# Two background streams for a pre-LN attention + MLP decode step with its gradients: groups of heads in one, weight gradients in the other

## The chip, the cores and the metric

One core of a Trainium2 chip. The metric is the device time of one execution in microseconds (us), the median of the runs of a kernel. All profiles quoted here fell in runs of the state "fast", and the ratios use fast runs alone; the medians are over all runs, of which a few are slow (three of 20 of d_two, one of four of d_wq_thin, and one run of the kernel before in three of the calls). One kernel's runs spread by 10 to 20 us, so I quote ratios to the kernel before from the same chip, with their 95% intervals. A ratio is the mean time of one kernel's fast runs over that of the other's of the same rounds, so it is not quite the ratio of the medians that I quote. A "point" is one per cent of the time of the kernel before.

In the profiles PE is the matmul engine (TensorE), PEld its loads of weights, DVE VectorE, ACT ScalarE and POOL GpSimd. The granted clock is the share of PE's full clock that the profile records as granted. Rounds and heads are counted from 0, from the start of a head's score maximum or of its first gV product; the prediction counts p1 heads from 1, so its head 34 is round 33 here.

## The reference, cut to what matters

```python
# B=2, Sq=1, D=640, 32 heads of 128, Sk=4096, Dff=1728; all bf16
def _A_ref(x, k_cache, v_cache, wq, wo):
    q = (x @ wq).reshape(B, Sq, Hq, Dh).transpose(0, 2, 1, 3)
    p = softmax(einsum("bhqd,bhkd->bhqk", q, k_cache) * Dh**-0.5)
    o = einsum("bhqk,bhkd->bhqd", p, v_cache)
    return o.transpose(0, 2, 1, 3).reshape(B, Sq, Hq * Dh) @ wo
h  = x + _A_ref(layernorm(x), k_cache, v_cache, wq, wo)
h2 = h + relu(layernorm(h) @ w1) @ w2
# returned: h2, and by jax.vjp the gradients of x, k_cache, v_cache, wq, wo, w1, w2
```

K and V are 67 MB each and their gradients as much; V is read twice, since the gradient of P needs the gradient of o, which needs the whole forward pass of its batch. In all 372.7 MB move.

## The kernel before: the parts that the change touches

The work on a head is cut into steps. "p1" (66 rounds i) reads K and V, makes the softmax and its sums; "p2" (64 heads j) reads V again (tile W), makes the gradients gV and gK and stores them. Between steps a list of background generators advances; each of their `yield`s has a price, and each step of p1 or p2 adds `rate` to a credit that pays for them. So a higher price makes background work thinner over the foreground.

```python
    bg = []
    done = set()
    credit = [0.0]

    def bg_one():

        while bg:
            try:
                said = next(bg[0][1])
            except StopIteration:
                done.add(bg[0][0])
                bg.pop(0)
                continue
            if isinstance(said, tuple):
                done.add(said)
            return said if isinstance(said, float) else 0.35
        return 0.0

    def bg_step(rate):
        credit[0] = credit[0] + rate if bg else 0.0
        while bg and credit[0] > 0.0:
            credit[0] -= bg_one()

    def bg_until(mark):
        while mark not in done:
            assert bg_one() > 0.0, mark

    M0_ITERS = 11
    P2_AT = H + 2 + M0_ITERS
    RATES = (0.2, 0.5, 0.12, 0.42, 0.88)
    # ... cut: two rounds i for each head j from round P2_AT on, then heads j alone
```

The middle of a batch (row products with wo, w1, w2, then the gradient of the attention output, head by head on VectorE), cut:

```python
    def middle_gen(b):
        # ... cut
        for c in range(ND):
            for h in range(H):
                nc.tensor.matmul(a_ps[:, c:c + 1], lhsT=wo_t[:, h, c * 128:(c + 1) * 128], rhs=OFc[:, h, b:b + 1],
                                 start=(h == 0), stop=(h == H - 1))
                if h % 8 == 7:
                    yield
        # ... cut: layer norm, w1, relu, gradient back to h
        for g in range(H // GH):                 # 4 groups of 8 heads
            for k in range(GH):
                ttr(wo_t[:, g * GH + k, :], hbc[:], go32[:, k:k + 1], D)     # DVE
                yield 0.9
            # ... cut: pr from go32 on DVE
            nc.tensor.matmul(d_ps[:, 0, :], lhsT=ones_f32[:], rhs=pr[:], start=True, stop=True)
            # ... cut
            yield ("go", b, g)                   # head j waits for its group
        # ... cut: product with w2, the row y
        yield ("y", b)
```

The weight gradients, one generator behind the middle of batch 1:

```python
    def fin_gen(fin):
        # ... cut: out_5, out_7, out_6 by outer_rows (matmul of 2-row operands, eviction, store)
        while ("go", 1, H // GH - 1) not in done:
            yield
        yield from rows_of(fin, GQc, H, HD, "GQr")
        yield from rows_of(fin, x1c, ND, D, "x1r")
        yield from outer_rows(fin, FIN["x1r"], D, FIN["GQr"], HD, out_4, ND)
        # ... cut
        for c in range(ND):
            while free["ld"] < 1:
                yield
            st = take("ld", [128, NSC, 128], "wqs")
            nc.sync.dma_start(out=st[:], in_=wqn[:, c, :].rearrange("p (h n) -> p h n", n=128))
            acc = pst([128, B], FP32, "m", "gx_ps")
            for g in range(H // GT):
                t_sb = transpose_group(st, g, g % 2 == 1)
                # ... cut
                yield
                for j in range(GT):
                    h = g * GT + j
                    nc.tensor.matmul(acc[:], lhsT=t_sb[:, j, :], rhs=GQc[:, h, :],
                                     start=(h == 0), stop=(h == H - 1))
                yield
        # ... cut: layer norm back, gradient of x
```

## Time and profile before

| | before |
|---|---|
| time | 1096.96 us median of 3 runs (1096.2 to 1105.84) |
| profiled run | 1104.41 us, trace 1102.6 us, granted clock 0.705 |
| moved | 372.70 MB, mean 338 GB/s |

From the page of the kernel before: the span in 40 equal slices, each digit the busy share in tenths, PEclk the granted TensorE clock in tenths, DMA the busy share of the 16 DMA engines.

```profile
PE   6999888999989878987983863663579788897574
...
PEclk9999899885597988798775565865555555555555
DMA  9999999895475889899899999999679999989835
```

The reader is to see three holes in the DMA row, at slices 10 to 13, around 29, and at the end, and that PE is at 8 or 9 in the first hole. The stretches behind these holes are in the prediction.

### The profile page before, as it was taken

How to read it: one execution, taken by the hardware profiler on the slowest of the kernel's cores; microseconds unless marked ns; L12 is line 12 of the kernel's file. 1: busy time of each engine (PE TensorE's matmuls, PEld its weight loads, DVE VectorE, ACT ScalarE, POOL GpSimd, SP SyncE). 2: the span in 40 equal slices, each digit the busy share in tenths (PEclk: the TensorE clock that was granted, in tenths of full speed). 3: DMA queues.
4: the chain of work that ended last, by engine and by line, in shares of the span. 5: the costliest groups of instructions: out<-in, count | busy, mean ns of one | idle time of the engine just before them, and what ended most of it. 6: DMA issues, size and time to landing. Idle time of an engine off the chain costs nothing.

```text
span 1102.6 us, 32287 instructions
## 1 busy us (share of the span) xinstructions
PE 867.1 (79%) x14111; PEld 748.6 (68%) x14111; DVE 717.6 (65%) x1694; ACT 634.7 (58%) x945; POOL 95.9 (9%) x216
## 2 busy tenths in 40 slices
PE   6999888999989878987983863663579788897574
PEld 5988888888878867876883752553556566554563
DVE  3666777763498876665665677788845665576345
ACT  4555555554566765775762763653367667665343
POOL 0000000000000000000001111111111111111001
PEclk9999899885597988798775565865555555555555
DMA  9999999895475889899899999999679999989835
GB/s 355 374 388 404 410 402 366 290 338 207 159 281 176 287 343 361 330 364 368 344 411 413 360 378 383 369 368 372 278 259 410 409 374 367 365 339 406 333 157 222
DMA packets 59757, 372.70 MB, mean 338 GB/s; under 512 B 5760, under 2 KB 15424, under 8 KB 17376
## 3 DMA queue, kind: packets, MB, share of 16 engines
q1 hardware_dynamic: 38960, 221.50, 53.6%
q0 software_dynamic: 20656, 149.14, 33.3%
q8 instruction: 110, 1.80, 0.6%
q14 instruction: 31, 0.25, 0.1%
HBM read 221.48 MB, written 149.13 MB: 336 GB/s over the span
## 4 chain that ended last, share of the span: by engine, by line
PE 41%; DMA 24%; DVE 17%; issue 10%; ACT 6%; POOL 1%; SPq 0%; POOLq 0%; ACTq 0%; DVEq 0%
PE t_ps L274 17%; DMA out_dram<-gV 10%; PE m_ps L304 9%; DMA Wt<-in_A_v_cache_dram 7%; DVE gK L545 5%; DVE pk L310 4%; PE m_ps L320 3%; PE o_ps L647 3%; ACT t_sb L279 3%; DVE junk L436 3%; PE s_ps L285 3%; DMA out_dram<-ot 2%; DVE gV L545 2%; DMA Vt<-in_A_v_cache_dram 2%; PE dp_ps L285 1%
## 5 line engine op out<-in xcount | busy, mean ns | idle before, releaser
L279 ACT COPY t_sb<-t_ps 128x1024 bf16<-128x1024 bf16 x489 | 490.3, 1014 | 242.8 <-PE t_ps L274 236.5
L274 PE MATMUL t_ps<-ident_bf,Wt 128*128 128x128 bf16 x2048 | 241.7, 291 | 17.3 <-DMA Wt<-in_A_v_cache_dram 16.8
L274 PEld LDWEIGHTS <-Wt 128*128 128x128 bf16 x2048 | 187.2, 133 | 62.3 <-issue 42.9
L285 PEld LDWEIGHTS <-t_sb 128*128 128x128 bf16 x4096 | 171.5, 104 | 61.3 <-ACT t_sb L279 51.2
L310 DVE TENSOR_TENSOR pk<-Kt,ep 128x1024 bf16<-128x1024 bf16 x256 | 174.9, 685 | 47.9 <-ACT ep L353 47.8
L304 PE MATMUL m_ps<-pk,Vt 128*128 128x129 bf16 x2048 | 199.3, 239 | 0.8 <-issue 0.7
L545 DVE TENSOR_TENSOR gV<-rb,pp 128x2048 bf16<-128x2048 bf16 x128 | 156.1, 1219 | 52.1 <-DMA out_dram<-gK 29.0
L274 PE MATMUL t_ps<-ident_bf,Kt 128*128 128x128 bf16 x2048 | 180.7, 240 | 10.7 <-DMA Kt<-in_A_k_cache_dram 9.0
L545 DVE TENSOR_TENSOR gK<-rb,gsp 128x2048 bf16<-128x2048 bf16 x128 | 154.1, 1218 | 37.9 <-DMA out_dram<-gV 37.8
L274 PEld LDWEIGHTS <-Kt 128*128 128x128 bf16 x2048 | 138.0, 107 | 12.7 <-DMA Kt<-in_A_k_cache_dram 10.3
L304 PEld LDWEIGHTS <-Vt 128*128 128x128 bf16 x2048 | 140.1, 106 | 6.8 <-issue 1.9
L285 PE MATMUL dp_ps<-goc,t_sb 128*128 128x1 bf16 x2048 | 97.6, 169 | 37.2 <-ACT t_sb L279 34.7
L589 POOL DMA_DIRECT2D out_dram<-gV x64 | 34.1, 534 | 730.2 <-DVE gV L545 696.0
L277 DVE COPY t_sb<-t_ps 128x1024 bf16<-128x1024 bf16 x43 | 29.7, 692 | 103.4 <-PE t_ps L274 100.7
L285 PE MATMUL s_ps<-qc,t_sb 128*128 128x1 bf16 x2048 | 90.0, 165 | 4.5 <-DVE gsp L580 1.6
L406 ACT ACTIVATE MT<-m_ps,rtot 128x128 bf16<-128x128 f32 x64 | 23.5, 367 | 114.6 <-PE m_ps L304 114.6
L320 PEld LDWEIGHTS <-Kt 128*128 128x128 bf16 x2048 | 64.9, 98 | 16.8 <-issue 15.2
L320 PE MATMUL m_ps<-ep,Kt 128*128 128x1 bf16 x2048 | 71.0, 164 | 6.0 <-ACT OU L407 6.0
L652 DVE CAST ot<-o_ps 128x128 bf16<-128x128 f32 (+2 forms) x80 | 33.4, 418 | 49.1 <-PE o_ps L647 42.0
L650 ACT CAST ot<-o_ps 128x512 bf16<-128x512 f32 (+1 forms) x80 | 47.0, 588 | 18.9 <-PE o_ps L647 9.3
L559 ACT CAST rb<-rb_ps 128x256 bf16<-128x256 f32 x64 | 24.1, 376 | 53.0 <-DVE gK L545 35.0
L605 POOL DMA_DIRECT2D out_dram<-gK x64 | 34.0, 531 | 232.9 <-DVE gK L545 200.7
(168 smaller groups left out, 747.3 us busy)
## 6 DMA issues: line engine op xcount, KB each, us to landing
Kt<-in_A_k_cache_dram SPq DMA_DIRECT2D x64, 1024.0 KB, 9.1
Vt<-in_A_v_cache_dram SPq DMA_DIRECT2D x64, 1024.0 KB, 7.9
Wt<-in_A_v_cache_dram SPq DMA_DIRECT2D x64, 1024.0 KB, 9.1
out_dram<-gV POOLq DMA_DIRECT2D x64, 1024.0 KB, 8.9
out_dram<-gK POOLq DMA_DIRECT2D x64, 1024.0 KB, 9.1
wo_t<-in_A_wo_dram SPq DMA_DIRECT2D x4, 1280.0 KB
out_dram<-ot POOLq DMA_DIRECT2D x5, 1024.0 KB, 12.8
wqs<-in_A_wq_dram SPq DMA_DIRECT2D x5, 1024.0 KB, 7.1
```

Source lines behind the costliest of these rows:

```text
L274: nc.tensor.transpose(t_ps[:, j, :], nat[:, g * GT + j, :], ident_bf[:])
L279: nc.scalar.copy(out=t_sb[:], in_=t_ps[:])
L285: nc.tensor.matmul(dst[:, sc:sc + 1], lhsT=t_sb[:, j, :], rhs=vec, start=True, stop=True)
L304: nc.tensor.matmul(r["m"][:, 0:129], lhsT=r["V"][:, sc, :], rhs=r["pk"][sc // GT][:, sc % GT, 0:129], start=False, stop=(sc == NSC - 1))
L310: nc.vector.tensor_tensor(out=pk[:, :, 0:128].rearrange("p s (a two) -> p s a two", two=2), in0=p["K"][:, sl, :].rearrange("p s (a two) -> ...
L320: nc.tensor.matmul(r["m"][:, 129:130], lhsT=r["K"][:, sc, :], rhs=r["ep"][:, sc, 0:1], start=(sc == 0), stop=False)
L436: nc.vector.tensor_tensor_reduce(out=junk[0:kc, 0:width], in0=in0, in1=in1, scale=1.0, scalar=0.0, op0=ALU.mult, op1=ALU.add, accum_out=acc)
L545: nc.vector.tensor_tensor(out=pairs_view(dst[:, sl, :]), in0=row.rearrange("p (a two) -> p a two", two=2)[:, None, :, :].to_broadcast([128 ...
L589: nc.gpsimd.dma_start(out=natural(out_3, b, h), in_=gV[:])
L605: nc.gpsimd.dma_start(out=natural(out_2, bp, hp), in_=gK[:])
L650: nc.scalar.copy(out=ot[0:P, k, n0:n0 + nn], in_=o_ps[0:P, 0:nn])
L652: nc.vector.tensor_copy(out=ot[0:P, k, n0:n0 + nn], in_=o_ps[0:P, 0:nn])
```

## The change

Its intent: the four groups of heads of a batch no longer stand before the row y. Group 0 comes first, then y, then groups 1 to 3; the weight gradients run in a second stream that starts as soon as y of batch 1 is there. The middle of batch 0 is spread over 15 p1 heads, not 11, in smaller steps and at a higher price (0.5 a step, not 0.35). The part through wq moves ahead of out_4, with one tile loaded ahead and a price of 0.9 + 0.5 per eight transposes, not 0.35 + 0.35. Three of four evictions go to ScalarE. The weights are loaded at heads 7, 11, 16, 20, 24, 28, and a further generator of the first stream, ga_gen, starts at round 12, not 14.

```diff
-                if h % 8 == 7:
+                if h % (4 if b == 0 else 8) == 3:
                     yield
...
-        for g in range(H // GH):
-            ... (the body is now go_group(b, g, hbc))
+        yield from go_group(b, 0, hbc)
...
         yield ("y", b)
+        for g in range(1, H // GH):
+            yield from go_group(b, g, hbc)
...
-                    if fw[0] % 2:
+                    if fw[0] % 4:
                         nc.scalar.copy(out=ot[0:P, k, n0:n0 + nn], in_=o_ps[0:P, 0:nn])
...
-                    yield 0.5
+                    yield 0.55
...
-        (rows_of GQr, rows_of x1r, outer_rows out_4: moved behind the gradient of x)
+        nxt = None
+        for c in range(-1, ND):
+            st = nxt
+            if c + 1 < ND:
+                while free["ld"] < 1:
+                    yield
+                nxt = take("ld", [128, NSC, 128], "wqs")
+                nc.sync.dma_start(out=nxt[:], in_=wqn[:, c + 1, :].rearrange("p (h n) -> p h n", n=128))
+            if c < 0:
+                for _ in range(8):
+                    yield
+                continue
...
                 t_sb = transpose_group(st, g, g % 2 == 1)
-                yield
+                yield 0.9
...
-            return said if isinstance(said, float) else 0.35
+            return said if isinstance(said, float) else 0.5
...
-    M0_ITERS = 11
-    RATES = (0.2, 0.5, 0.12, 0.42, 0.88)
+    M0_ITERS = 15
+    RATES = (0.2, 0.5, 0.15, 0.46, 0.3)
+    RATE2 = 0.9
...
+    W_AT = (7, 11, 16, 20, 24, 28)
-        if ii is not None and 8 <= ii < 26 and ii % 3 == 0:
-            queue.append(("w", (5, 4, 0, 1, 2, 3)[(ii - 8) // 3]))
+        if ii in W_AT:
+            queue.append(("w", (5, 4, 0, 1, 2, 3)[W_AT.index(ii)]))
...
-            bg.append(("fin", fin_gen(fin)))
+            bg2.append(("fin", fin_gen(fin)))
-        if i == 14:
+        if i == 12:
             bg.append(("ga", ga_gen()))
...
-                bg_step(rate)
+                bg_step(0, rate)
+                bg_step(1, RATE2)
```

More of the change, by code (lines that the diff above doesn't have):

```diff
@@ L440, in one, with go_group @@
         return src[:, :, b]
+    def go_group(b, g, hbc):
+        hs = slice(g * GH, (g + 1) * GH)
+        go32 = small.tile([128, GH], FP32, tag="go32", bufs=1, name="go32")
+        for k in range(GH):
+            ttr(wo_t[:, g * GH + k, :], hbc[:], go32[:, k:k + 1], D)
+            yield 0.9
+        nc.vector.tensor_copy(out=goc[:, hs, b], in_=go32[:])
+        pr = small.tile([128, GH], FP32, tag="pr", bufs=1, name="pr")
+        nc.vector.tensor_tensor(out=pr[:], in0=goc[:, hs, b], in1=OU[:, b, hs, 0], op=ALU.mult)
+        yield
+        yield
+        d_ps = pst([128, 2, GH], FP32, "mid", "d_ps")
+        nc.tensor.matmul(d_ps[:, 0, :], lhsT=ones_f32[:], rhs=pr[:], start=True, stop=True)
+        for k in range(GH):
+            h = g * GH + k
+            nc.tensor.matmul(d_ps[:, 1, k:k + 1], lhsT=MTs.pop((b, h))[:], rhs=goc[:, h, b:b + 1],
+                             start=True, stop=True)
+        nc.vector.tensor_scalar(out=negdot[:, hs, b], in0=d_ps[:, 0, :], scalar1=-1.0, scalar2=None, op0=ALU.mult)
+        ud = small.tile([128, GH], FP32, tag="ud", bufs=1, name="ud")
+        nc.vector.tensor_tensor(out=ud[:], in0=OU[:, b, hs, 1], in1=negdot[:, hs, b], op=ALU.mult)
+        nc.vector.tensor_tensor(out=ud[:], in0=d_ps[:, 1, :], in1=ud[:], op=ALU.add)
+        nc.vector.tensor_scalar(out=GQc[:, hs, b], in0=ud[:], scalar1=SCALE, scalar2=None, op0=ALU.mult)
+        yield ("go", b, g)
     def middle_gen(b):
@@ L489, in middle_gen @@
         yield ("gh1", b)
-        for g in range(H // GH):
-            hs = slice(g * GH, (g + 1) * GH)
-            go32 = small.tile([128, GH], FP32, tag="go32", bufs=1, name="go32")
-            for k in range(GH):
-                ttr(wo_t[:, g * GH + k, :], hbc[:], go32[:, k:k + 1], D)
-                yield 0.9
-            nc.vector.tensor_copy(out=goc[:, hs, b], in_=go32[:])
-            pr = small.tile([128, GH], FP32, tag="pr", bufs=1, name="pr")
-            nc.vector.tensor_tensor(out=pr[:], in0=goc[:, hs, b], in1=OU[:, b, hs, 0], op=ALU.mult)
-            yield
-            yield
-            d_ps = pst([128, 2, GH], FP32, "mid", "d_ps")
-            nc.tensor.matmul(d_ps[:, 0, :], lhsT=ones_f32[:], rhs=pr[:], start=True, stop=True)
-            for k in range(GH):
-                h = g * GH + k
-                nc.tensor.matmul(d_ps[:, 1, k:k + 1], lhsT=MTs.pop((b, h))[:], rhs=goc[:, h, b:b + 1],
-                                 start=True, stop=True)
-            nc.vector.tensor_scalar(out=negdot[:, hs, b], in0=d_ps[:, 0, :], scalar1=-1.0, scalar2=None, op0=ALU.mult)
-            ud = small.tile([128, GH], FP32, tag="ud", bufs=1, name="ud")
-            nc.vector.tensor_tensor(out=ud[:], in0=OU[:, b, hs, 1], in1=negdot[:, hs, b], op=ALU.mult)
-            nc.vector.tensor_tensor(out=ud[:], in0=d_ps[:, 1, :], in1=ud[:], op=ALU.add)
-            nc.vector.tensor_scalar(out=GQc[:, hs, b], in0=ud[:], scalar1=SCALE, scalar2=None, op0=ALU.mult)
-            yield ("go", b, g)
+        yield from go_group(b, 0, hbc)
         m_ps = pst([128, ND], FP32, "mid", "mlp_ps")
@@ L669, in fin_gen @@
             yield
-        yield from rows_of(fin, GQc, H, HD, "GQr")
-        yield from rows_of(fin, x1c, ND, D, "x1r")
-        yield from outer_rows(fin, FIN["x1r"], D, FIN["GQr"], HD, out_4, ND)
         gx1 = fin.tile([128, B, ND], FP32, tag="gx1", name="gx1")
         wqn = A_wq.rearrange("(c p) n -> p c n", p=128)
-        for c in range(ND):
-            while free["ld"] < 1:
-                yield
-            st = take("ld", [128, NSC, 128], "wqs")
-            nc.sync.dma_start(out=st[:], in_=wqn[:, c, :].rearrange("p (h n) -> p h n", n=128))
+        nxt = None
[3 more added lines that the diff above has]
+                while free["ld"] < 1:
+                    yield
+                nxt = take("ld", [128, NSC, 128], "wqs")
+                nc.sync.dma_start(out=nxt[:], in_=wqn[:, c + 1, :].rearrange("p (h n) -> p h n", n=128))
+            if c < 0:
+                for _ in range(8):
+                    yield
+                continue
             acc = pst([128, B], FP32, "m", "gx_ps")
@@ L684, in fin_gen @@
                     give("ld")
-                yield
+                yield 0.9
                 for j in range(GT):
@@ L698, in fin_gen, with bg_one @@
             yield
+        yield from rows_of(fin, GQc, H, HD, "GQr")
+        yield from rows_of(fin, x1c, ND, D, "x1r")
+        yield from outer_rows(fin, FIN["x1r"], D, FIN["GQr"], HD, out_4, ND)
     bg = []
+    bg2 = []
     done = set()
-    credit = [0.0]
-    def bg_one():
-        while bg:
+    credit = [0.0, 0.0]
+    def bg_one(q):
+        while q:
             try:
-                said = next(bg[0][1])
+                said = next(q[0][1])
             except StopIteration:
-                done.add(bg[0][0])
-                bg.pop(0)
+                done.add(q[0][0])
+                q.pop(0)
                 continue
@@ L715, in bg_one, with bg_step @@
                 done.add(said)
-            return said if isinstance(said, float) else 0.35
+            return said if isinstance(said, float) else 0.5
         return 0.0
-    def bg_step(rate):
-        credit[0] = credit[0] + rate if bg else 0.0
-        while bg and credit[0] > 0.0:
-            credit[0] -= bg_one()
+    def bg_step(k, rate):
+        q = (bg, bg2)[k]
+        credit[k] = credit[k] + rate if q else 0.0
+        while q and credit[k] > 0.0:
+            credit[k] -= bg_one(q)
     def bg_until(mark):
         while mark not in done:
-            assert bg_one() > 0.0, mark
-    M0_ITERS = 11
+            assert bg_one(bg) > 0.0, mark
+    M0_ITERS = 15
     P2_AT = H + 2 + M0_ITERS
-    RATES = (0.2, 0.5, 0.12, 0.42, 0.88)
+    RATES = (0.2, 0.5, 0.15, 0.46, 0.3)
+    RATE2 = 0.9
     plan = []
@@ L808 @@
                 pump()
-                bg_step(rate)
+                bg_step(0, rate)
+                bg_step(1, RATE2)
         if i is not None and i in (H + 1, NP1 + 1):
             bg.append((f"m{i // H - 1}", middle_gen(i // H - 1)))
-    while bg:
-        bg_one()
+    while bg2:
+        bg_one(bg2)
     fin.release()
```

## The prediction

> **What bounds the kernel now.** I read the span in 40 slices first, then the busy time by stretch, then the chain of waits, then the waits of single stretches. Work on the 64 K/V heads ("p1") is followed by work on the 64 gradient heads ("p2": read V once more, write gV and gK); for each time below I took the start of the head's score maximum (L394) or of its first gV product (L545) in the timeline. The stretches, as busy time by stretch (columns: us, busy us with instruction counts of PE, PEld, DVE, ACT, POOL, then granted clock, DMA share, GB/s):
>
> ```profile
> 70.00:185.00 115.00, 104.60 (x2211) 96.64 (x2208) 81.28 (x267) 63.87 (x117) 0.00 (x0) 0.94 1.02 401
> 185.00:248.00 63.00, 58.45 (x1167) 54.19 (x1166) 44.81 (x148) 34.62 (x63) 0.00 (x0) 0.89 0.88 317
> 248.00:306.00 58.00, 54.38 (x906) 50.62 (x903) 25.93 (x100) 29.50 (x50) 0.00 (x0) 0.53 0.54 191
> 306.00:355.00 49.00, 42.99 (x829) 39.62 (x829) 41.53 (x144) 31.10 (x52) 0.00 (x0) 0.86 0.67 238
> ...
> 391.00:565.00 174.00, 145.40 (x2797) 133.94 (x2798) 112.65 (x289) 114.61 (x172) 11.75 (x27) 0.85 0.91 354
> 565.00:741.00 176.00, 105.33 (x1688) 92.78 (x1688) 122.45 (x195) 94.52 (x115) 26.09 (x60) 0.59 0.96 380
> 741.00:801.00 60.00, 30.56 (x461) 27.36 (x459) 51.70 (x96) 23.08 (x28) 10.19 (x21) 0.54 0.81 326
> 801.00:953.00 152.00, 132.64 (x1194) 94.08 (x1193) 90.62 (x133) 106.99 (x159) 24.79 (x56) 0.50 0.94 365
> 953.00:1010.00 57.00, 47.48 (x402) 29.83 (x402) 36.44 (x44) 35.63 (x52) 9.83 (x22) 0.50 0.95 369
> 1010.00:1088.00 78.00, 53.49 (x682) 45.83 (x682) 35.87 (x58) 34.99 (x41) 7.06 (x16) 0.50 0.63 250
> ```
>
> Where the DMA share is 0.94 or more, transfers bound the kernel. Three stretches fall out: 248 to 355 (middle of batch 0, PE nearly always busy), 741 to 801 (the four groups of heads of batch 1, DVE busy 51.7 of 60) and 1010 to 1088 (gradient of x, nothing saturated). The waits of the last two say why. The first two lines are from 741 to 801, the rest from 1010 to 1103 (total us, times, longest):
>
> ```profile
> PEld d_ps L502 <- DVE pr L498: 23.2, 3, 9.6
> PE d_ps L502 <- DVE pr L498: 22.9, 3, 9.6
> ```
>
> ```profile
> ACT t_sb L279 <- PE t_ps L274: 40.1, 23, 9.2
> DVE t_sb L277 <- PE t_ps L274: 31.4, 9, 11.3
> ...
> PEld L274 <- DMA wqs<-in_A_wq_dram: 8.9, 1, 8.9
> PEld L688 <- ACT t_sb L279: 8.7, 8, 1.4
> PEld L688 <- DVE t_sb L277: 8.6, 9, 1.1
> PE t_ps L274 <- DMA wqs<-in_A_wq_dram: 8.4, 1, 8.4
> ```
>
> In the first, PE stands for a whole group's reductions on DVE, three times some 8 us. In the second, the transposes of wq stand directly behind their own load, and then PE and the copies wait for each other in turn: five gradient heads take 78 us there instead of 8.8 us each (20 heads in 176 us, 565 to 741).
>
> [...] the page agrees, with 53.6% (loads) and 33.3% (stores) of the same 16 engines, so an earlier weight gradient can only fill DMA time that gradient heads leave. [...] the 22.9 us and 8.4 us above are what a not yet ready matmul costs all behind it. [...] The stretches after 801 show 0.50 throughout; I assume that it stays so there.
>
> **The change part by part.** Instruction counts on PE hardly change (28173 rows of the program's order in both): it is a matter of placement. I go by the program's order of the changed kernel, cut at each head.
>
> Weights evenly: the same 9.7 MB, the last two quarters of wo at heads 24 and 28 in place of 21 and 24. From 70 to 185 DMA is full (401 GB/s); from 185 to 248 it has room (317). 2.6 MB at 401 GB/s are 6.5 us; PE, busy 58 of 63 us in the later stretch, gives part back. I take 4 us: head 34 starts at 244 instead of 248.
>
> Middle of batch 0: before, 11 p1 heads alone (to 355), then pairs of two p1 and one p2. The change has 15 alone. Before, heads 34 to 37 carried 219, 203, 173 and 175 matmuls and took 10.0, 11.7, 12.8, 12.6 us (clock 0.5 to 0.6). After: 159, then 163 four times, 137, 181, 165, 131 three times, 137, 131, 131, 210. Plain p1 heads of 131 matmuls took 6.2 us at full clock and about 7.5 where it dipped; 203 at half clock took 11.7, or 57 ns each. So five of about 163 at 8.7 = 43.5, one 7.5, one 9.5, one 9, three 22, three 24, the last 11: 126 us (244 to 370). Before, the same fifteen took 248 to 391, 143 us, but had gradient heads 0 and 1 in them. Two more heads alone cost 2 x 8.8 = 17.6 later. Net 143 against 144: **nothing gained in this part by itself**.
>
> Pairs: heads 49 to 65 with nine gradient heads in both, 391 to 565 before: 174 us, kept. Only matmul counts of the small groups move. End at 544, with gradient head 9 next (before: 565, head 11).
>
> Heads 9 to 31: 22 x 8.8 = 194, to 738 (before: 741). The middle of batch 1 lies in it in both; these heads are DMA-bound (0.96), so its changed grain is hidden.
>
> From head 31 to the end, 361 us before. After, only group 0 is needed before the row y, so the weight gradients start at head 32, not 38, at about 8 row-chunks a head (9 before); groups 1 to 3 go beside them, at heads 35, 41, 47, not in a burst. The wq part comes at heads 50 to 55 with one load ahead, and out_4 fills 58 to 62. Sum:
> head 31, 8.8; head 32 (37 row matmuls more), 12; heads 33 to 48, bound by DMA: 16 x 3.15 MB and 9.6 MB of gradients are 60 MB, at the 390 GB/s I get for heads 39 to 52 before (53 MB in 136 us) 154, and 4 more for heads 41 and 46 with row matmuls; head 49, 8.5; heads 50 to 55: 114 to 122 matmuls each; before, heads 59 to 61 had 486 in 48.3 us, 0.099 us each, so 686 are 68, and 3 for the handoffs; head 56, 9; head 57, 12; heads 58 to 62, five at 9.2 (before, heads 55 and 56 of like content took 9.0 and 8.7) 46; head 63 and the drain 14.6 as before. Together about 340. What it removes: most of the 60-us DVE-bound stretch's excess, some 8 us, the 15.6 us head at which the gradients began, and 78 us becoming five heads of 9.2. What it adds: 71 us for the six heads that now carry wq, where plain ones take 53. Evictions move to ACT (three of four, not one of two): per head about 4.1 + 0.4 + 3.5 = 8.0 us of ACT, still under 9.2.
>
> End: 738 + 340 = 1078 on the trace. The trace of before is 1102.6 against a median of 1096.96, so 5.6 less: 1072. I round it to **1070 us**.
>
> **The rivals.** First, the gain is larger: p2 is fully bound by transfers, and everything else hides. From head 31 then 33 x 3.15 + 20.4 = 124 MB at 390 GB/s are 319, and 12 for the end: 331, and with 8 us won in the middle of batch 0 the time is near 1055. For it: 420 GB/s in single heads. Against it: PE at clock 0.5, busy 133 of 152 us from 801, is the next bound. Second, ACT or the two PSUM banks become a new wait: both streams use the same bank "mid" (d_ps and o_ps), and t_sb copies queue behind three quarters of the evictions. If each of some 26 such heads loses 0.6 us, 16 us go and the time is 1086. Third, the middle of batch 0 costs: four more p1 heads alone with PE bound and DMA at 0.6 cannot be won back if they take 9.7 us as before; 15 x 9.7 = 145 in place of 126 makes it 1089.
>
> **Range and chances.** The terms: start +-4, middle +-9, the end +-12, independent, so about 15; low 1051, high 1089. Faster by over 2% is below 1075.5, 0.37 of a deviation above the centre: 0.63. Within 2%: 0.36. Slower: 0.01.
>
> **What would show it.** Gradient head 9 starting near 544 and head 31 near 738; the stretch from head 31 to 48 with DMA at 0.94 or more and no wait of several us of d_ps on pr; no wait of PE for wqs; heads 50 to 55 at 11 to 12 us; 8 to 10 us a head for out_4; the last stores within 15 us of head 63. It is wrong if PE's clock does not stay 0.5, if the waits of PE for ACT's t_sb grow in the last third, or if p1 heads 34 to 48 take over 9 us each.

## The result

| | before | after |
|---|---|---|
| median of 4 runs | 1096.58 us (1095.19 to 1105.84) | 1048.11 us (1044.91 to 1056.89) |
| ratio | 1 | 0.9554, interval 0.9473 to 0.9634 |
| trace | 1102.6 us | 1044.0 us |
| mean GB/s | 338 | 357 |

It is faster by 4.5%, below my range. From the page of the changed kernel, the same rows as those of before:

```profile
PE   6999989999998988878895665547998987676795
...
PEclk9988999899969889887875575566555555667555
DMA  9999999999857578898999999999899998999697
```

The first hole is shallower, the one at three quarters has gone, and the end is better filled. The stretches of the changed kernel, cut at heads as in the prediction (busy time by stretch; columns: us, busy us with counts of PE, PEld, DVE, ACT, POOL, then granted clock, DMA share, GB/s):

```profile
185.00:247.00 62.00, 57.56 (x1201) 53.05 (x1199) 44.62 (x151) 36.47 (x67) 0.00 (x0) 0.94 0.94 351
247.00:280.00 33.00, 33.00 (x809) 31.35 (x809) 18.49 (x67) 24.30 (x39) 0.00 (x0) 1.00 0.92 325
280.00:317.00 37.00, 34.56 (x645) 31.53 (x642) 20.68 (x84) 25.57 (x43) 0.00 (x0) 0.77 0.67 242
317.00:363.00 46.00, 40.15 (x818) 37.10 (x819) 38.34 (x134) 28.45 (x47) 0.00 (x0) 0.90 0.70 251
363.00:532.00 169.00, 143.16 (x2770) 133.07 (x2767) 122.14 (x321) 114.96 (x176) 11.75 (x26) 0.86 0.87 337
532.00:718.00 186.00, 110.75 (x1783) 99.26 (x1784) 129.23 (x198) 96.75 (x118) 29.16 (x67) 0.58 0.98 390
...
735.00:886.00 151.00, 134.79 (x1246) 97.34 (x1246) 101.92 (x165) 111.65 (x183) 26.84 (x60) 0.50 0.96 383
886.00:956.00 70.00, 50.49 (x816) 46.30 (x817) 41.40 (x51) 41.38 (x48) 9.69 (x22) 0.70 1.01 419
956.00:980.00 24.00, 13.53 (x142) 10.73 (x138) 11.61 (x24) 11.92 (x17) 2.61 (x6) 0.50 0.81 326
980.00:1028.00 48.00, 46.58 (x382) 27.81 (x380) 30.66 (x36) 37.39 (x57) 8.65 (x19) 0.50 0.79 318
```

Two lines matter most. From 247 to 280 PE does five heads of the middle at clock 1.00 with the DMA share at 0.92; before, the first five heads of the middle ran at 0.53 and 0.54 (with more of the middle in them: the product with w1 too). From 886 to 956 the wq part stands inside gradient heads with DMA at 1.01 and 419 GB/s; before, it ran from 1010 to 1088 at 0.63. In the waits from 718 to 886 there is none left of d_ps on pr. In those from 886 to 956 none is on the wqs load either; the longest waits of PE and PEld that remain of that part, and below them the time from issue to landing of the wqs loads:

```profile
PEld L697 <- DVE t_sb L277: 12.9, 6, 5.2
PE gx_ps L697 <- DVE t_sb L277: 12.3, 6, 5.1
```

```profile
DMA to landing us min/median/max: 17.4/17.4/17.4
```

The trace has the landing of only one of the five wqs loads: 17.4 us (18.2 in the control), against a median of 7.1 of three before. On the page of the changed kernel the queue of the loads has 56.2% and that of the stores 34.7% of the same 16 engines' span, and from 886 to 956 the DMA share is 1.01. That the load took longer because V and the stores moved beside it is my estimate, not shown by a run; no wait of PE for wqs is left here, as it is issued a tile ahead.

### The profile page after: what moved, and what is told of

It is laid out like the page before. It is cut to its first block, busy times and chain, and to the rows that moved or that the text cites.

```text
span 1044.0 us, 32292 instructions
## 1 busy us (share of the span) xinstructions
PE 843.8 (81%) x14111; PEld 730.7 (70%) x14111; DVE 698.8 (67%) x1654; ACT 644.8 (62%) x985; POOL 95.2 (9%) x216
## 3 DMA queue, kind: packets, MB, share of 16 engines
q1 hardware_dynamic: 38960, 221.50, 56.2%
q0 software_dynamic: 20656, 149.14, 34.7%
## 4 chain that ended last, share of the span: by engine, by line
PE 40%; DMA 26%; DVE 16%; issue 10%; ACT 5%; POOL 1%; SPq 0%; POOLq 0%; ACTq 0%; DVEq 0%
PE t_ps L274 16%; DMA out_dram<-gV 15%; PE m_ps L304 9%; DMA Wt<-in_A_v_cache_dram 6%; DVE pk L310 5%; DVE gK L550 4%; PE o_ps L652 4%; PE m_ps L320 4%; PE s_ps L285 3%; DVE junk L436 3%; ACT t_sb L279 2%; DMA Vt<-in_A_v_cache_dram 2%; DMA Kt<-in_A_k_cache_dram 2%; PE dp_ps L285 1%; DVE gV L550 1%
## 5 line engine op out<-in xcount | busy, mean ns | idle before, releaser
L274 PE MATMUL t_ps<-ident_bf,Wt 128*128 128x128 bf16 x2048 | 239.2, 289 | 16.6 <-DMA Wt<-in_A_v_cache_dram 15.3
L304 PE MATMUL m_ps<-pk,Vt 128*128 128x129 bf16 x2048 | 193.3, 234 | 0.0
L274 PE MATMUL t_ps<-ident_bf,Kt 128*128 128x128 bf16 x2048 | 172.9, 234 | 2.3 <-DMA Kt<-in_A_k_cache_dram 2.3
L304 PEld LDWEIGHTS <-Vt 128*128 128x128 bf16 x2048 | 135.8, 104 | 4.5
L274 PEld LDWEIGHTS <-Kt 128*128 128x128 bf16 x2048 | 132.4, 104 | 3.6 <-DMA Kt<-in_A_k_cache_dram 2.7
L406 ACT ACTIVATE MT<-m_ps,rtot 128x128 bf16<-128x128 f32 x64 | 23.5, 368 | 105.3 <-PE m_ps L304 105.3
L320 PEld LDWEIGHTS <-Kt 128*128 128x128 bf16 x2048 | 64.7, 97 | 20.3 <-issue 18.9
L655 ACT CAST ot<-o_ps 128x512 bf16<-128x512 f32 (+3 forms) x120 | 59.8, 526 | 11.7 <-PE o_ps L652 10.4
L436 DVE CUSTOM_DVE_ANT_0 junk<-wo_t,hbc 128x640 bf16<-128x640 bf16 x64 | 52.1, 815 | 0.1
## 6 DMA issues: line engine op xcount, KB each, us to landing
Wt<-in_A_v_cache_dram SPq DMA_DIRECT2D x64, 1024.0 KB, 10.6
wqs<-in_A_wq_dram SPq DMA_DIRECT2D x5, 1024.0 KB, 17.4
```

The source lines that it names most:

```text
L274: nc.tensor.transpose(t_ps[:, j, :], nat[:, g * GT + j, :], ident_bf[:])
L304: nc.tensor.matmul(r["m"][:, 0:129], lhsT=r["V"][:, sc, :], rhs=r["pk"][sc // GT][:, sc % GT, 0:129], start=False, stop=(sc == NSC - 1))
L320: nc.tensor.matmul(r["m"][:, 129:130], lhsT=r["K"][:, sc, :], rhs=r["ep"][:, sc, 0:1], start=(sc == 0), stop=False)
L436: nc.vector.tensor_tensor_reduce(out=junk[0:kc, 0:width], in0=in0, in1=in1, scale=1.0, scalar=0.0, op0=ALU.mult, op1=ALU.add, accum_out=acc)
L655: nc.scalar.copy(out=ot[0:P, k, n0:n0 + nn], in_=o_ps[0:P, 0:nn])
```

## The experiments

Eighteen runs, in five calls, each on one chip: u_wq, u_mid, u_one and u_w; then c_after, m_burst8, m_hf and e_pad; then d_wq, d_two, d_mid and e_pad4; then t_dense, d_wq_thin, d_both and u_ev; then c_after5 and e_pad4w. Only the second and the last hold the changed kernel itself as a control; in the others it is compared by way of the ratio to before. "Undo" runs take one part out of the changed kernel, "alone" runs put one part into the kernel before.

| run | what | ratio to before | interval |
|---|---|---|---|
| c_after | changed kernel, control | 0.9569 | 0.9489 to 0.9649 |
| c_after5 | the same, 5 rounds | 0.9546 | 0.9505 to 0.9588 |
| u_wq | undo: wq last, no load ahead | 0.9626 | 0.9582 to 0.9671 |
| u_mid | undo: 11 heads and steps of 8 | 0.9596 | 0.9550 to 0.9641 |
| u_one | undo: one stream | 0.9692 | 0.9635 to 0.9748 |
| u_w | undo: places of the weights | 0.9495 | 0.9444 to 0.9546 |
| u_ev | undo: share of evictions | 0.9580 | 0.9522 to 0.9638 |
| m_burst8 | 15 heads, steps of 8 | 0.9649 | 0.9552 to 0.9746 |
| m_hf | half steps of the w1 product too | 0.9663 | 0.9576 to 0.9751 |
| t_dense | wq dense | 0.9646 | 0.9613 to 0.9679 |
| d_wq | alone: wq early, load ahead, dense | 0.9965 | 0.9941 to 0.9988 |
| d_two | alone: second stream | 0.9969 | 0.9942 to 0.9997 |
| d_mid | alone: 15 heads, steps of 4 | 0.9970 | 0.9942 to 0.9998 |
| d_wq_thin | alone: wq early, load ahead, thin | 0.9859 | 0.9808 to 0.9911 |
| d_both | second stream and thin early wq | 0.9730 | 0.9691 to 0.9768 |
| e_pad | all gradient rows padded | 0.9630 | 0.9541 to 0.9718 |
| e_pad4 | only the rows of out_4 padded | 0.9514 | 0.9437 to 0.9590 |
| e_pad4w | that, and the weights at the old places | 0.9491 | 0.9449 to 0.9532 |

### Undoing one part

My theory was that each part removes its own wait, so that each comes back when its part is undone. The rival was that transfers bound everything else, so that a part's gain is made up elsewhere.

u_wq puts out_4 ahead of wq again and loads each wq tile just before its use; the prices stay.

```diff
-        nxt = None
-        for c in range(-1, ND):
-            ... (load one tile ahead)
+        for c in range(ND):
+            while free["ld"] < 1:
+                yield
+            st = take("ld", [128, NSC, 128], "wqs")
+            nc.sync.dma_start(out=st[:], in_=wqn[:, c, :].rearrange("p (h n) -> p h n", n=128))
```

> The changed kernel with one part undone: the gradient of x through wq stands last again (after out_4) and each wq tile is loaded just before its transposes, not one tile ahead. Theory (the order and the load ahead are worth most of the last third): PE waits for wqs again, 5 to 9 us for the first tile, and the heads that carry it (55 to 61) run with the DMA share under 0.8 because the loads of V are over; 12 to 25 us slower than the changed kernel, 1060 to 1073. Rival (a second stream at a thin rate is enough, order does not matter): within 5 us of the changed kernel, 1043 to 1053.

Median 1060.06 us. The waits of u_wq from 953 to its end:

```profile
PE t_ps L274 <- DMA wqs<-in_A_wq_dram: 23.5, 4, 7.5
```

PE's queue stands four times for a load, 23.5 us in all. The end came 0.6 to 0.8 points later than in the controls. The theory held in kind. In size it fell short: by the ratios 6 to 9 us, not 12 to 25, and the heads with wq (55 to 61) ran at a DMA share of 0.86, not under 0.8.

u_one puts the groups before y again and the weight gradients behind them in one stream.

```diff
-        yield from go_group(b, 0, hbc)
+        for g in range(H // GH):
+            yield from go_group(b, g, hbc)
...
-        for g in range(1, H // GH):
-            yield from go_group(b, g, hbc)
...
-            bg2.append(("fin", fin_gen(fin)))
+            bg.append(("fin", fin_gen(fin)))
...
-    RATES = (0.2, 0.5, 0.15, 0.46, 0.3)
+    RATES = (0.2, 0.5, 0.15, 0.46, 1.1)
```

> The changed kernel with one background stream: all four groups of heads before the row y, then the weight gradients behind them, at rate 1.1 so that they still end by head 62. Theory (starting the gradients at head 32 and spreading the groups gives some 10 us): PE waits on pr for d_ps again, 15 us or more in all, heads 32 to 37 run at a DMA share of about 0.8, 8 to 14 us slower than the changed kernel, 1056 to 1062. Rival (that is made up later because the rest is bound by transfers): within 4 us.

Median 1065.03 us. Its waits from 722 to 797:

```profile
PE d_ps L455 <- DVE pr L451: 24.6, 3, 11.2
```

The wait of the kernel before (22.9 us) is back, and 1.2 to 1.5 points with it, by the ratios 13 to 16 us, a little over what I expected. The rate had to change with the streams (1.1 for one, in place of 0.3 and 0.9), which is in this number. Of the parts that were undone singly this is the largest.

u_mid takes the middle back to 11 heads and steps of 8, and m_burst8 keeps the 15 heads but takes steps of 8.

```diff
# u_mid
-                if h % (4 if b == 0 else 8) == 3:
+                if h % 8 == 7:
-    M0_ITERS = 15
+    M0_ITERS = 11
# m_burst8
-                if h % (4 if b == 0 else 8) == 3:
+                if h % 8 == 3:
```

> The changed kernel with the middle of batch 0 over 11 heads and the wo product in steps of 8 as before (56 to 64 small matmuls in heads 34 to 36, not 28 to 32). Theory (thin steps keep PE's clock at 1.00, that is the 10 us that I missed): the clock falls to about 0.5 in heads 34 to 38 and these take 10 to 12 us, not 6.7; gradient head 9 is reached 10 to 15 us later relative to the changed kernel, 1056 to 1065. Rival (the middle is neutral, as my prediction said: what it takes from one stretch it gives to another): 1043 to 1053.

> The changed kernel with 15 heads for the middle of batch 0, but the wo product in steps of 8 (heads 34 to 36 carry 52, 64 and 44 small matmuls, not 28 to 32). Theory (small steps keep the clock full): clock near 0.5 in heads 34 to 36, 9 to 11 us each and not 6.7, about 8 us later at head 38; of this at most half is left at the end. Rival (the clock falls at random, whatever the steps): heads 34 to 38 as in the changed kernel, 6.7 us at clock 1.00.

Medians 1056.51 and 1056.85 us. Rounds 33 to 35 hold the product with wo alone. As busy time by stretch: the changed kernel, m_burst8, and d_mid, a run described further below, which puts 15 heads and steps of 4 into the kernel before at its old price of 0.35.

```profile
247.00:267.00 20.00, 20.00 (x490) 18.98 (x490) 11.48 (x43) 14.72 (x25) 0.00 (x0) 1.00 0.92 329
```

```profile
247.00:268.00 21.00, 20.97 (x540) 19.93 (x536) 11.06 (x42) 14.18 (x24) 0.00 (x0) 1.00 0.87 308
```

```profile
246.00:275.00 29.00, 28.05 (x500) 26.62 (x500) 11.56 (x40) 14.12 (x22) 0.00 (x0) 0.55 0.67 227
```

So the size of the steps does not part these clocks: m_burst8 carries 44, 64 and 52 small matmuls in these rounds, the changed kernel 28, 32 and 32, and both keep 1.00; d_mid carries 32, 48 and 44 in steps of 4 and falls to 0.55. What parts the traces is a wait, here of the kernel before from 248 to 251 (the same line stands in d_mid):

```profile
PE a_ps L448 <- DVE OFc L443: 1.2, 1, 1.2
```

At a price of 0.35 and a rate of 0.5 the first products follow DVE's copy of their operand (OFc) within one step, and PE waits 1.2 us for the copy. At 0.5 the copy uses up the credit of the step, and the products come a step later. All six traces with the old price (before, d_wq, d_two, d_mid, d_wq_thin, d_both) have this wait; the clock is at 0.5 within 0.9 to 3.1 us after it (in the kernel before it is 1.00 to 250.3 us, 0.96 us after the wait, and 0.51 from 250.3 to 251), and rounds 33 to 35 take 29 to 35 us at 0.53 to 0.59. None of the 14 with the new price has it; they take 20 to 25 us at 0.80 to 1.00. No run changes the price alone, so that the wait brings the clock down is argued, not shown; and not every pause does: in c_after PE stood for 1.15 us at 264 us and the clock stayed at 1.00.

My mark, round 38, was not a fair one. By then m_burst8 has also done the product with w1 (0.59 from 268 to 288 us), which the changed kernel does in rounds 39 and 40, at 0.60 and 0.55. From round 33 to round 43, behind both products, m_burst8 took 80.8 us, the changed kernel 78.0 and its control 79.4. At the end the intervals of m_burst8 and the control overlap, but in the raw times all four runs of m_burst8 (1051.42 to 1059.4) lie above all four of the control (1046.31 to 1051.2); what costs it these us is open. u_mid reached head 11 at 554 us, the changed kernel at 555: more gradient heads lie in its pairs. Counted from round 33, which stands before every change of the middle, that is 312 against 308 us (311 in both controls), and 317 in the kernel before. u_mid, which keeps the new price, lost 0.3 to 0.5 points at the end, not clear of the controls' intervals.

m_hf makes the steps of the w1 product smaller as well.

```diff
-            if cf % 2 == 1:
-                yield
+            yield
```

> The changed kernel with the w1 product of both middles also in steps half as large (heads 40 to 42 carry 25, 40 and 18 small matmuls, not 50 and 34). Theory of small steps: clock 0.9 or more in heads 39 to 42 where the changed kernel has 0.60, 0.55, 1.00, 0.78, and each about 7 us, not 9.7 to 10.4; 5 to 8 us earlier at head 43, 0 to 6 us less at the end. Rival: those heads stay at 9 to 10 us, no change.

Median 1059.58 us: no gain; its four runs lie above all four of the control. Heads 39 to 42 did keep their clock (0.95 from 291 to 324 us, where the changed kernel has 0.73 from 287 to 325), but in u_wq, which leaves these steps alone, they had 0.91, so the smaller steps are not shown to do it. The credit of the 15 heads was used up by the extra steps, so the product with w2 came later, its 70 matmuls from 366 to 380 us and not from 358 to 364, and the clock fell there: 0.57 from 361 to 389 us. Thin has to fit into the rounds that there are.

u_w and u_ev take back the places of the weights and the share of evictions.

```diff
# u_w
-        if ii in W_AT:
-            queue.append(("w", (5, 4, 0, 1, 2, 3)[W_AT.index(ii)]))
+        if ii is not None and 8 <= ii < 26 and ii % 3 == 0:
+            queue.append(("w", (5, 4, 0, 1, 2, 3)[(ii - 8) // 3]))
# u_ev
-                    if fw[0] % 4:
+                    if fw[0] % 2:
```

> The changed kernel with the weights at the old places (heads 9, 12, 15, 18, 21, 24). Prediction's 4 us against what the trace of the changed kernel shows at head 34 (about 1 us): I expect 0 to 2 us slower, 1046 to 1051; the theory of even loading as worth 4 us or more would show 1052 or more, with head 34 about 4 us later.

> The changed kernel with every second eviction of the weight gradients on DVE, not every fourth. DVE is busy 0.67 and ACT 0.80 of heads 58 to 62, PE 0.98. Theory (PE bounds these heads, so either engine will do): within 3 us of the changed kernel, 0.953 to 0.959. Rival (it relieves DVE where the outer products need it): 4 to 8 us slower.

Medians 1044.41 and 1049.41 us: neither part is a gain that these runs show. u_w was at 0.9495, below both controls; but the first 33 rounds, in runs that have the same instructions there, ended anywhere from 241 to 247 us, and u_w's 241 lies in that.

> The changed kernel once more, unaltered but for an empty line at its end, as the control of this call: 0.955 of the kernel before, give or take 0.006, and with that the spread between executions that a part has to clear. Its first 33 heads are the same instructions as in all runs that undo a later part; their traces reach head 33's maximum at 241 to 247 us, and I expect this one within that.

Median 1049.08 us, round 33 at 244: as expected.

### One part alone in the kernel before

```diff
# d_wq: the part through wq before out_4, one tile loaded ahead, old prices (0.35 + 0.35)
# d_two: go_group(b, 1..3) behind y, weight gradients in a second stream at rate 0.9 (old prices, wq last, no load ahead)
# d_mid
-                if h % 8 == 7:
+                if h % (4 if b == 0 else 8) == 3:
-    M0_ITERS = 11
+    M0_ITERS = 15
```

> The kernel before with one part alone: the gradient of x through wq ahead of out_4, with one wq tile loaded ahead. Theory (the tail of before, heads 58 to 63 at 78 us, was a wait of PE for a load and for copies with transfers idle): wq falls to heads 54 to 57 where loads of V still fill the transfers, no PE wait for wqs of over 2 us, the DMA share from head 54 to the end rises from about 0.7 to over 0.85; 14 to 25 us faster than before, 0.977 to 0.987 of it. Rival (the tail is bound by PE at clock 0.50 wherever it stands): within 6 us, 0.995 or more.

> The kernel before with one part alone: groups 1 to 3 after the row y, and the weight gradients in a second stream at rate 0.9 from head 31 (not 38), wq still last and without a load ahead. It ends its gradients at head 55 and leaves eight plain heads. Theory (two streams fill the DVE-bound stretch of 60 us, and an earlier end takes the tail along): no d_ps wait on pr over 5 us, heads 31 to 38 below 62 us with gradients in them; 20 to 32 us faster, 0.971 to 0.982. Rival (the second stream only moves the work, PE at 0.50 bounds it): within 8 us.

> The kernel before with one part alone: 15 heads for the middle of batch 0 and steps of 4 (but the old price of a step, so that heads 34 to 36 carry 44 to 48 small matmuls). My prediction said of this part: nothing by itself. Theory now (two more gradient heads stay behind to hide the rest, and the clock holds up): 4 to 10 us faster, 0.991 to 0.996. Rival (neutral): 0.997 to 1.003.

Medians 1094.62, 1096.94 and 1093.49 us of 20 runs each, against 1099.24: 0.3% each. For d_wq and d_two my theory missed the near end of what it expected by some 10 and 17 us; d_mid fits its rival (neutral), but at the old price it still has the wait for OFc and a clock of 0.53 in rounds 33 to 37, so it is not the changed kernel's middle by itself. Undone from the changed kernel these parts cost more than they give alone, so a sum of separate waits is not the whole cause. The stretches show what stands in the way. d_wq: its wq part in four heads, then its out_4.

```profile
961.00:1025.00 64.00, 40.37 (x576) 35.46 (x577) 28.69 (x48) 27.02 (x31) 5.56 (x14) 0.61 0.90 348
1025.00:1081.00 56.00, 50.86 (x421) 31.13 (x421) 38.05 (x46) 37.32 (x57) 8.68 (x19) 0.50 0.68 275
```

d_two, its wq part:

```profile
933.00:1013.00 80.00, 44.28 (x607) 37.71 (x605) 30.00 (x47) 28.88 (x33) 5.90 (x14) 0.56 0.74 284
```

In d_wq the part has its load ahead and V still to read, and yet heads 54 to 56 take 20.3, 15.0 and 14.2 us (8.8 was plain), and PE still waits 6.7 us for wqs. In d_two, without a load ahead, 20.7 us of PEld's waits are for wqs, and heads 51 to 54 take 80 us. (Its trace fell in a run 9 us under its median. It was at head 31 at 729 us against 741, but 6 of these us stood at round 33, before any change.) The full ones of these heads carry 48 to 56 transposes of wq. In the changed kernel it is 24 to 32 by the program's order. That was a new theory: not where wq stands but how dense it is decides, and thin takes six heads, for which only an early start has room.

### The density of the wq part

```diff
# t_dense (changed kernel)
                 t_sb = transpose_group(st, g, g % 2 == 1)
-                yield 0.9
+                yield 0.35
...
-                yield
+                yield 0.35
# d_wq_thin (d_wq)
-                yield
+                yield 0.9
# d_both (changed kernel): M0_ITERS = 11, steps of 8, price 0.35 in the first stream, its rates
#   and the places of the weights as before, ga_gen at round 14
```

> The changed kernel with the wq part as dense as before: 48 to 56 transposes in each of heads 50 to 52, in place of 24 to 32 in each of heads 50 to 55; order, load ahead and second stream kept. Theory (thinness is what hides wq): heads 50 to 52 take 15 to 20 us each with a DMA share that falls, and three plain heads are left at the end; 8 to 18 us slower than the changed kernel, 0.963 to 0.971 of before. Rival (early end and load ahead suffice): within 4 us, 0.952 to 0.960.

> The kernel before with wq ahead of out_4, one tile loaded ahead, and thin (24 to 32 transposes a head) but with one stream, so that 22 of 40 row-chunks of out_4 fall behind the last gradient head. Theory (thin needs the early start): heads 54 to 59 take 9 to 12 us each, but 15 to 25 us of out_4 stand alone at the end; 0.990 to 1.000 of before. Rival (thinness alone is the gain): 0.980 or less.

> The changed kernel without its middle of batch 0 and without its places of the weights, or the kernel before with the second stream and the thin, early wq together. Theory (these two belong together and are nearly all of the gain): 0.957 to 0.966 of before, where each alone gave 0.997. Rival (all parts share the gain about evenly): 0.970 or more.

Medians 1057.03, 1082.03 and 1065.58 us, against 1095.15. t_dense, its heads 50 to 52:

```profile
894.00:947.00 53.00, 34.83 (x498) 30.91 (x496) 21.35 (x29) 22.80 (x25) 3.94 (x9) 0.56 0.94 372
```

Three heads in 53 us, 17.8 each, against six in 64 us (10.6 each) from 892 to 956 in the changed kernel. The DMA share fell less than I expected (0.94, and 372 GB/s against 419). Density alone costs 0.8 to 1.0 points, with order, load ahead and second stream kept. PE is busy 35 of 53 us. The program sends transposes, copy and matmul through two PSUM buffers one after the other; in this stretch the copies wait 43.8 us for the transposes (ACT 23.6, DVE 20.2) and PE waits 17.2 us for the copies before its gx_ps matmuls (8.9 for DVE's, 8.3 for ACT's). That what a head does meanwhile is too little to fill those gaps is my estimate from these waits; no run here widens the buffers.

d_wq_thin, six heads with wq, then from the start of head 63 to its end:

```profile
947.00:1013.00 66.00, 44.24 (x718) 40.99 (x718) 37.90 (x55) 35.60 (x41) 8.31 (x20) 0.68 0.99 411
...
1049.00:1075.60 26.60, 15.76 (x89) 6.39 (x86) 14.64 (x20) 10.40 (x15) 3.19 (x6) 0.50 0.73 297
```

The six heads now have DMA at 0.99 and 411 GB/s, as in the changed kernel, and 22 of 40 chunks of out_4 hang over the end: 26.6 us after the start of the last head, where the changed kernel needs 16. The result, 0.9859, lies between what the two theories gave. Thin is a gain by itself (d_wq had 0.9965). The missing early start takes part of it. PE also waited 11.7 us for wqs in these heads, although it is loaded one tile ahead; what that cost was not tested.

d_both, 0.973, was over what I gave for "nearly all of the gain" and fits the rival: second stream and thin early wq are some 2.7 of 4.5 points. The rest needs the first stream's part. Its middle, five heads:

```profile
246.00:302.00 56.00, 52.65 (x903) 49.34 (x903) 25.41 (x99) 29.01 (x47) 0.00 (x0) 0.57 0.55 194
```

This is the kernel before (0.53 and 0.54 there). From d_both (0.973) to u_mid (0.9596) lie the price 0.5, the first stream's rates, the start of ga_gen and the places of the weights, of which u_w shows no gain by the last. I did not take price and rates apart. The traces point to the price: d_both has the wait for OFc and takes 56 us for rounds 33 to 37, u_mid has not and takes 44. Of these 12 us, 6 are left at head 11 (318 against 312 from round 33).

### The clock of the last third

In the changed kernel PE is busy 46.6 of 48 us from 980 to 1028 at clock 0.50. The matmuls of the weight gradients have 2 of 128 rows. e_pad gives their row operands 128 partitions, zeros but for two, cleared on GpSimd; e_pad4 does so for out_4 alone and clears early.

```diff
-        r = pool.tile([B, n * 128], BF16, tag=name, name=name)
+        r = PAD[name] if name in PAD else pool.tile([B, n * 128], BF16, tag=name, name=name)
...
+        PAD["GQr"] = fin.tile([128, HD], BF16, tag="GQr", name="GQr")
+        PAD["x1r"] = fin.tile([128, D], BF16, tag="x1r", name="x1r")
+        for k in range(4):
+            nc.gpsimd.memset(PAD["GQr"][:, k * HD // 4:(k + 1) * HD // 4], 0.0)
+            yield 0.01
+        nc.gpsimd.memset(PAD["x1r"][:], 0.0)
```

> The changed kernel whose weight gradients multiply rows padded with zeros from 2 to 128 partitions (same results, same matmul widths; the padding is cleared on GpSimd). It asks why PE stays at clock 0.50 in the last third although it is 97% busy from 980 to 1028. Theory [...]: the clock rises over 0.8 in the stretch of out_4, its heads take 8 us, not 9.2, and the time falls by 3 to 10 us. Rival [...]: clock 0.50 as before, time within 3 us or up to 5 us longer by the clearing.

> The changed kernel with only the rows of out_4 padded with zeros to 128 partitions, cleared when the gradients start. From the run with all rows padded (clock 0.88 and 7.4 us a head in out_4, but slower at heads 31 to 57 where the clearing stands in the stores' queue). Theory: heads 59 to 62 at 7.2 to 7.6 us, clock over 0.85, everything before head 57 as in the changed kernel; 4 to 9 us less than it, 0.946 to 0.952 of before. Rival (the end is then set by something else, ACT at 0.97 or the last stores): within 2 us of the changed kernel, 0.953 to 0.958.

Heads 59 to 62 of the changed kernel, as a stretch and as its group of out_4 matmuls (busy us, mean ns of one, idle before):

```profile
991.00:1028.00 37.00, 36.65 (x303) 21.90 (x301) 24.79 (x30) 29.32 (x44) 7.35 (x16) 0.50 0.90 368
```

```profile
L652 PE MATMUL o_ps<-GQr,x1r 2*128 2x512 bf16 x32 | 17.7, 616 | 0.4
```

The same heads of e_pad4:

```profile
993.00:1023.00 30.00, 23.63 (x299) 16.78 (x300) 25.04 (x30) 28.38 (x45) 7.47 (x17) 0.91 1.01 413
```

```profile
L653 PE MATMUL o_ps<-GQr,x1r 128*128 128x512 bf16 x30 | 11.3, 406 | 5.0 <-ACT ot L656 2.6 <-DVE ot L658 1.4
```

The same widths with 128 rows instead of 2: the clock is 0.91, a matmul takes 406 ns, not 616, and a head 7.4 us, not 9.2. DMA is then at 1.01 and 413 GB/s, with ACT busy 28.38 and PE 23.63 of 30 us; which of DMA and ACT is then the bound was not tested. e_pad showed the same clock effect (0.88 in its heads 58 to 62) but its time was 0.963: it lost it again between heads 31 and 58, where the clearing of all rows stands before their use. Its heads 31 and 32 took 10.0 and 11.9 us, against 9.7 and 7.4 in the changed kernel (8.0 and 8.9 in the control), and head 41 took 13.9 against 8.5. That the clearing is the cause there is argued, not shown.

The last call sets the control beside both changes that had looked better, on one chip with five rounds.

> The changed kernel unaltered, as the control on the same chip: 0.955 to 0.958 of before.

> The changed kernel with the rows of out_4 padded to 128 partitions and with the weights at the old places. Theory (each is worth about 4 us, as the single runs hinted): 0.945 to 0.951 of before and an interval that lies below the control's middle. Rival (the end is given back by other waits, the places are noise): 0.953 to 0.958, within 2 us of the control. In either case heads 59 to 62 at 7.2 to 7.7 us.

Medians 1048.76 and 1041.16 us, ratios 0.9546 and 0.9491. The second interval ends at 0.9532, below the control's 0.9546, but the two intervals overlap; in raw times five of its six runs (1039.51 to 1041.87) lie under all six of the control (1044.53 to 1052.9), and one (1050.32) does not. It is the fastest kernel by its median, faster than before by 5%; that it beats the changed kernel is likely, not shown beyond the spread.

## Why the prediction was wrong

"Faster" was right, at a chance of 0.63, and of what would show it the removed waits came true: none of d_ps on pr, none on wqs, and with them heads 50 to 55 at 10.6 us on average, out_4 at 9.2 us a head, head 63 and the end in 16 us. But a sign of being wrong came true as well: PE's clock did not stay at 0.5 (0.70 from 886 to 956), and in the middle of batch 0 it was 1.00 where the sum took half of it. The size was off: heads 9 and 31 came at 532 and 718 us, not 544 and 738, and 1048.11 us lies 3 us under the range. On the trace my sum was 1078, and 1044 was measured. No single term holds these 34 us: the middle of batch 0 was 10 us shorter, heads 31 to 48 11, heads 9 to 31 8, heads 50 to 55 7 and the pairs 5; the start and the end were 7 longer. By terms:

| term of the sum | predicted | measured | |
|---|---|---|---|
| to round 33 | 244 | 247 | spread of runs: 241 to 247 |
| middle of batch 0, 15 heads | 126 | 116 | clock 1.00 in five heads |
| pairs | 174 | 169 | not tested |
| heads 9 to 31 | 194 | 186 | 8.45 a head, not 8.8 |
| head 31, heads 32 to 48 | 8.8 + 170 | 9.7 + 158 | row heads |
| heads 50 to 55 | 71 | 64 | clock 0.71, not 0.50 |
| the other heads and the drain | 90 | 94 | |

- **Middle of batch 0.** The step that failed is "five of about 163 at 8.7". I took the mean of full and half clock, as before had it (0.89 from 185 to 248 us, 0.53 from 248 to 306). In the changed kernel the same heads took 6.7 us at clock 1.00, which is 10 us. I had looked at how many small matmuls a head gets; the traces part instead by the wait of 1.2 us for OFc, which the old price brings and the new one does not (argued from 20 traces, see above). "Nothing gained in this part by itself" failed too, in the place where the rest is done: d_both, without the first stream's part, stood at 0.973, the changed kernel at 0.9546 to 0.9569, so this part is worth 1.6 to 1.8 points there. u_mid, which undoes heads and steps but not price and rates, lost only 0.3 to 0.5 of them; the price and the rates were missing from my sum.
- **Heads 31 to 48.** Head 32 took 7.4 us, not 12: 18 of the 37 row matmuls fell into head 31, and the two together took 17.1 us, not 20.8. The later heads with row matmuls (40 and 45 in the trace) did take 11.8 and 14.5 us, and yet the 16 heads took 151 us, not 154 + 4. The prediction shows no trace for its 12; in the kernel before the head with these matmuls, 38, took 15.6 us. Why they cost less beside a first stream was not tested.
- **Heads 50 to 55.** "I assume that it stays so there" (clock 0.50) failed: it was 0.71 from 892 to 956 us, with DMA at a share of 1.01 and 420 GB/s. I had also called stretches at a DMA share of 0.94 bound by transfers (365 GB/s from 801 to 953); 1.01 and 420 GB/s here say that this was not the limit. My rate of 0.099 us for each matmul came from dense heads. The density, which I had read from the program's order as 24 to 32 transposes instead of 48 to 56, was the point, and t_dense measures it: 17.8 us a head against 10.6. I treated it as a mere spreading.
- **Heads 9 to 31.** I took 8.8 us from 20 heads of before. PE's waits there for the operands of single small matmuls (15.5 and 12.3 us for sums of the layer norms, 7.9 for d_ps) are smaller in the changed kernel (6.1, 8.6, 4.8), and the two first heads, which refill the buffers, may weigh less among 22. None of this was tested by itself, so it stays open.
- **From trace to time.** I took 5.6 us off, because the trace of before fell in a run of 1104.41 us. The trace of after fell in a run 2.4 us under its median. So the two traces differ by 58.6 us and the medians by 48.5; the difference is spread of runs, and it hid a part of my error.
- **The rivals.** The first, "everything else hides", was nearest: its 1055. The second did not come about: ACT is busy 37 of 48 us at the end and u_ev, which relieves it, changes nothing. The third did not come about either.

What is shown and what is not: that the second stream and the density of wq cost 0.8 to 1.5 points when undone is shown (their intervals lie above that of the five-round control). They were run at other times. For order and load ahead of wq the 23.5 us of waits are shown, and the 0.6 to 0.8 points in time all but clear (0.9582 against 0.9588). That they depend on each other is shown: the second stream alone gives 0.3 points (d_two), the thin early wq 1.4 (d_wq_thin), both 2.7 (d_both). How the 1.3 points between d_both and u_mid fall on price and rates is open; the wait for OFc speaks for the price.

## What to carry to other kernels

When several parts remove waits in a row, each alone may be worth little and all of them much (here three were worth 0.3% each, the whole change 4.5%); judge a part in the place where the rest is already done. For work that goes back and forth between engines, look at its density beside the foreground as well as at its order: here 48 to 56 transposes a head took 17.8 us a head and 24 to 32 took 10.6, and the wq part early but dense was worth 0.35 points alone (d_wq, 0.9965), early and thin 1.4 (d_wq_thin, 0.9859). It had to be thin enough to hide, and started early enough to be thin. Before a PE stretch is called bound, look at the granted clock, and at what PE did just before it fell. Here it was 0.50 in heads 59 to 62 of the changed kernel with operands over 2 rows and 0.91 in the same heads of e_pad4 with operands over 128, and in the middle of batch 0 of the kernel before it fell from 1.00 to 0.5 within 1 us after PE had waited 1.2 us for DVE; in c_after it stayed at 1.00 after a pause of 1.15 us, so that the wait brings it down is not shown.
